# Two experts' second weights loaded in uneven row pieces, with tiny transfers between them

## The chip, the cores and the metric

The kernel runs on one core of a Trainium2 chip. The metric is the device time of one execution in microseconds (us): the median before is 178.28 us over three runs (178.04 to 178.61). A core has a matrix engine (TensorE, PE in the profile), a vector engine (VectorE, DVE), an activation engine (ScalarE, ACT), GpSimd (POOL), a queue engine (SyncE, SP), and 16 DMA engines that move data between the chip's main memory and the on-chip buffer of 128 partitions (rows).

## The reference

The reference does windowed attention for a batch of 8 with 8 heads, 576 positions and head size 64. Heads 0 to 3 see a plain window of 32 positions, heads 4 to 7 see 32 positions with a step of 4. The attention output is read as 4608 rows `x` of 512, and goes through a "soft" mixture of 8 experts with 4 slots each:

```
logits = x @ phi                       # 4608 x 32
d = softmax over the rows;  slot_input = d.T @ x     # 32 slots x 512
for e in range(8):                     # 4 slots of expert e
    h = relu(slot_input[e] @ w1[e])    # 512 -> 1024
    slot_out[e] = h @ w2[e]            # 1024 -> 512
c = softmax over the slots;  out = c @ slot_out      # 4608 x 512
```

All inputs and the output are float32 in main memory. The weights `w1` and `w2` take 2 MB per expert each, 33.6 MB together.

## The kernel before, in words

The work has two stages. First the attention of the eight batches, software-pipelined: a list of small steps written out by hand (`ORDER`) is run once per iteration, each step for the batch that its stage number gives. TensorE does scores, products and transposes, ScalarE the exponentials and many copies, VectorE the masks, 32x32 transposes and normalizations. Along the way the sums for the slots are collected. Then, once, the experts run on the 32 slots (`hps` at L608, `so` at L641), and the result is multiplied out to the 4608 output rows (L664), scaled on ScalarE and VectorE by turns (L673, L677), and stored (L686, L713).

Nearly all transfers are issued by GpSimd (`nc.gpsimd.dma_start`), in program order on one queue, and convert float32 to float16 on the way in. Every one of them covers 128 partitions, or 64 in the two last stores. In order: the raw q, k and v of each batch (L201, 1.2 MB of float32 each), with the weights `w1` of experts 0 to 4 put between them one at a time (L207), then `w1` of experts 5 to 7 as one transfer (L207), `w2` of experts 0 to 2 as one transfer (L212), `w2` of experts 3 to 5 as one transfer (L212, into space that the raw buffers leave), and `w2` of experts 6 and 7 in column halves (`load_half`, L220: one transfer per half for expert 6, two for expert 7). Last come the 17 stores of the output. The tile for `w2` of experts 0 to 2 is `w_0`; partition p holds, for each expert, 8 rows of `w2` one after the other, 4096 numbers, 16 KB in main memory and 8 KB on chip.

The list of weights that are loaded early is `EARLY`, and `load_weights` (L483) takes it off from the front. Its last entry, `(2, 0, 3)`, is the transfer that the change touches. It is issued when the raw v of the last batch has been issued (`loads`, L527). Completion of GpSimd's transfers is counted on eight semaphores, taken in turn: a transfer that comes to a semaphore waits, on GpSimd, until the one eight places before it has landed. The 16 DMA engines each write one completion mark of 4 bytes per transfer.

The order in which the experts are used is fixed at L690 to L708: experts 0 to 3, then 4 and 5, then the first column half of 6 and 7, then the first column half of the first output batches, with the second half of experts 6 and 7 put between them.

Of the kernel before, what the change touches and what calls it, by code (L numbers as in the profile page):

```python
# [10 lines left out]
FP16 = mybir.dt.float16  # L11
# [13 lines left out]
DMODEL = H * D  # L25
E_EXP = 8
S_PER_E = 4
N_SLOTS = 32
# [16 lines left out]
    (("P", 3), ("P", 4), ("L", 0), ("L", 1), ("D", 0)),  # L45
    (("D", 1), ("D", 2), ("D", 3)),
)
ORDER = """
MD0.2 MK2.2 AP4.2 ET.3 VBc.1 S1.1 MK0.1 RP4.2 ED.3 E1.1 AD1.2 EP.3 VC.1 RD1.2 MP4.2
VCc.1 ER.3 MD1.2 AD3.2 VA.1 QT0.0 AP3.2 RD3.2 VAc.1 QT1.0 RP3.2 MD3.2 S2.1 KT1.0  # L50
# [3 lines left out]
"""  # L54
STEPS = [(w.split(".")[0], int(w.split(".")[1])) for w in ORDER.split()]
ON_ACT = ('D3', 'P0', 'P1', 'P3')
# [40 lines left out]
def kernel(  # L97
# [10 lines left out]
    nc = tc.nc  # L108
# [5 lines left out]
    consts = ctx.enter_context(tc.tile_pool(name="consts", bufs=1))  # L114
# [3 lines left out]
    ident = cst[:, o : o + 128]  # L118
    spread = cst[:, o + 128 : o + 256]
    quad = cst[:, o + 256 : o + 260]  # L120
    masks = consts.tile([128, NMASK], FP16, name="masks")
    phi_raw = consts.tile([128, 4, N_SLOTS], FP16, name="phi_raw")
    phi4 = consts.tile([128, 4, 4, N_SLOTS], FP16, name="phi4")
# [14 lines left out]
    def weights_tile(pool, which, e0, e1):  # L138
        n = (4 * FDIM, 8 * DMODEL)[which - 1]
        t = pool.tile([128, e1 - e0, n], FP16, name=f"w{which}_{e0}", tag=f"w{which}_{e0}")  # L140
        for e in range(e0, e1):
            of = t[:, e - e0]
            if which == 1:
                w1t[e] = of.rearrange("p (c f) -> p c f", c=4)
            else:
                w2t[e] = of.rearrange("p (c n) -> p c n", c=8)
        return t

    EARLY = [(1, e, e + 1) for e in range(5)] + [(1, 5, 8), (2, 0, 3)]
    early_tiles = {x: weights_tile((w1_pool, w2a_pool)[x[0] - 1], *x) for x in EARLY}  # L150
# [54 lines left out]
    def load_full(t, which, e0, e1):  # L205
        if which == 1:
            nc.gpsimd.dma_start(  # L207
                out=t.rearrange("p e (u x) -> p (e u) x", u=2),
                in_=moe_w1[e0:e1].rearrange("e (u p c) f -> p (e u) (c f)", u=2, p=128),
            )  # L210
        else:
            nc.gpsimd.dma_start(  # L212
                out=t, in_=moe_w2[e0:e1].rearrange("e (p c) n -> p e (c n)", p=128)
            )

    def load_half(e, s, n):
        src = moe_w2[e].rearrange("(p c) n -> p c n", p=128)
        cols = slice(DH * s, DH * s + DH)
        for u in range(0, 8, n):
            nc.gpsimd.dma_start(out=w2t[e][:, u : u + n, cols], in_=src[:, u : u + n, cols])  # L220
# [249 lines left out]
    for which in "QK":  # L470
        load_raw(which, 1)
    nc.gpsimd.dma_start(
        out=phi_raw.rearrange("p (u c) s -> p u (c s)", u=2),
        in_=moe_phi.rearrange("(u p c) s -> p u (c s)", u=2, c=2),
# [8 lines left out]
    def load_weights(n):  # L483
        for _ in range(n):
            x = weights.pop(0)
            load_full(early_tiles[x], *x)

    tmp = {}

# [37 lines left out]
    def loads(which, b):  # L527
        load_raw(which, b)
        if which == "V":
            if b > 2:  # L530
                load_weights(1)
            if b == B - 1:
                load_weights(len(weights))
# [6 lines left out]
    for it in range(B + max(s for _, s in STEPS)):  # L540
        for op, stage in STEPS:
            b = it - stage
            if not 0 <= b < B:
                continue
            step(op, b)
            if op in frees and b + 2 < B:
                loads(frees[op], b + 2)
            left.discard((op, b))
            if w2b_pool is None and not left:
                raw_pool.release()  # L550
                w2b_pool = tc.alloc_tile_pool(name="w2b", bufs=1, side="right")
                late = weights_tile(w2b_pool, 2, 3, 6)
                slab_weights(6, "qk0", QK_SLAB)
                slab_weights(7, "qk1", QK_SLAB)
                load_full(late, 2, 3, 6)
                for s in range(2):
                    for e in (6, 7):
                        load_half(e, s, 8 if e == 6 else 4)
        if it == 0:
            nc.vector.tensor_copy(  # L560
                out=phi4, in_=phi_raw[:, :, None, :].broadcast_to([128, 4, 4, N_SLOTS])
            )
# [40 lines left out]
    for fc in range(2):  # L603
        for g in range(2):
            for dc in range(4):
                for j in range(4):
                    e = 4 * g + j
# [9 lines left out]
    for c in range(8):  # L617
# [3 lines left out]
        out=hTm[:, 0].rearrange("p c (j s) -> p c j s", j=4)[:, :, :, 0:16], in_=hT4[:, :, :, 0:16]  # L621
    )
    nc.scalar.copy(
        out=hTm[:, 1].rearrange("p c (j s) -> p c j s", j=4)[:, :, :, 16:32], in_=hT4[:, :, :, 16:32]
# [87 lines left out]
    for e in range(2):  # L712
        nc.gpsimd.dma_start(  # L713
            out=rest[:, e, 512:576, :].rearrange("n i d -> i n d"), in_=om_l[64 * e : 64 * e + 64]
# [37 lines left out]
```

## Time and profile before

| | |
|---|---|
| Median of three runs | 178.28 us |
| Profiled execution, its own time | 178.29 us |
| Its span (first to last instruction) | 176.5 us |
| Around the span | 1.79 us |
| TensorE / VectorE / ScalarE / GpSimd busy | 70% / 71% / 70% / 22% |
| Packets of GpSimd's queue | 18816, 40.41 MB written |
| Read from main memory / written to it | 62.07 MB / 9.44 MB |

The profile is one execution. "DMA" in its slices is the mean busy share of the 16 DMA engines. Each transfer of 128 rows is cut into packets, the same number for each DMA engine; an engine's packets follow each other without a hole as long as its queue holds work. Each transfer has 16 completion marks in the trace, one from each engine, and it has landed with the last of them. The trace does not number the engines: it tells that 16 marks came, and when, but not from which engine each came.

### The profile page before, as it was taken

The page shows a single profiled execution, that of the slowest core. Times are in us where ns is not written, and L with a number is a line of the kernel's source. Part 1 is how long each engine was busy: PE and PEld are TensorE (multiplying, and loading weights), DVE is VectorE, ACT ScalarE, POOL GpSimd, SP SyncE. Part 2 cuts the span into 40 slices and gives each one's busy share as a digit, 9 for nine tenths or more (in the row PEclk, how much of TensorE's full clock was granted, in tenths as well). Part 3 has the DMA queues.
Part 4 walks back from the last instruction along what each step waited for, and adds up shares of the span by engine and source line. Part 5 has one row for each costly group of instructions (what it writes and reads, how often), then busy time and mean ns, then how long its engine had stood idle before and what let it go on. Part 6 is the DMA issues. An engine that isn't in the chain of part 4 may idle for free.

```text
span 176.5 us, 4724 instructions
## 1 busy us (share of the span) xinstructions
PE 123.5 (70%) x2004; PEld 80.9 (46%) x2004; DVE 126.0 (71%) x275; ACT 123.5 (70%) x266; POOL 38.4 (22%) x60
## 2 busy tenths in 40 slices
PE   0026928998888888988989888978677295778300
PEld 0015616676566566656766557656332142221000
DVE  6473899999999999999999998465130104878500
ACT  6007758999999999999999999995501104888300
POOL 7321022112112112116000002710000001856600
PEclk9999999969999999999789999996858969655555
DMA  5999999999999999999999999999999999999997
GB/s 83 215 214 210 214 212 215 215 213 214 216 212 217 211 218 215 208 215 220 213 211 217 213 218 216 222 210 225 213 213 221 192 198 175 340 398 397 401 415 209
DMA packets 18981, 40.83 MB, mean 231 GB/s; under 512 B 1169, under 2 KB 11537, under 8 KB 18193
## 3 DMA queue, kind: packets, MB, share of 16 engines
q0 software_dynamic: 18816, 40.41, 113.8%
q8 instruction: 15, 0.25, 0.5%
q1 hardware_dynamic: 144, 0.14, 0.3%
q14 instruction: 6, 0.04, 0.1%
HBM read 62.07 MB, written 9.44 MB: 405 GB/s over the span
## 4 chain that ended last, share of the span: by engine, by line
ACT 38%; DMA 27%; DVE 14%; PE 10%; issue 2%; POOL 2%; POOLq 0%; ACTq 0%
DMA w<-in_moe_w_dram 19%; ACT p L282 10%; DMA phi_raw<-in_moe_phi_dram 8%; ACT vX L253 7%; ACT xp L337 7%; DVE qk L231 5%; PE f L664 5%; ACT om L673 3%; ACT xT L376 3%; ACT xT L378 3%; DVE p L293 3%; DVE vT L231 3%; ACT xd L337 2%; PE s L273 2%; PE rp L357 2%
## 5 line engine op out<-in xcount | busy, mean ns | idle before, releaser
L282 ACT ACTIVATE p<-s 128x1920 f16<-128x1920 f32 (+1 forms) x24 | 44.6, 1857 | 10.2 <-PE s L273 10.1
L273 PE MATMUL s<-qk 32*128 32x128 f16 (+2 forms) x704 | 26.7, 295 | 18.4 <-DVE qk L231 12.0
L253 ACT COPY vX<-rv 128x768 f16<-128x768 f16 (+1 forms) x32 | 27.8, 943 | 1.8 <-PE rv L247 1.8
L316 PEld LDWEIGHTS <-p 128*128 128x128 f16 (+1 forms) x480 | 22.4, 103 | 13.3 <-DVE xp L341 4.0
L337 ACT ACTIVATE xp<-o_P,rc_P 128x64 f16<-128x64 f32 x96 | 26.5, 497 | 2.2 <-DVE rc_P L328 2.2
L273 PEld LDWEIGHTS <-qk 32*128 32x128 f16 x704 | 17.3, 117 | 21.6 <-DVE qk L231 12.0
L293 DVE TENSOR_TENSOR p<-p,masks 128x1920 f16<-128x1920 f16 (+1 forms) x24 | 25.7, 1084 | 0.2
L231 DVE STREAM_TRANSPOSE qk<-rawQ 128x576 uint32<-128x576 uint32 x16 | 18.8, 1243 | 2.7 <-DMA rawQ<-in_q_dram 2.7
L316 PE MATMUL o_P<-vX,p 128*128 128x65 f16 (+1 forms) x288 | 20.0, 205 | 0.8 <-ACT xp L337 0.2
L231 DVE STREAM_TRANSPOSE qk<-rawK 128x576 uint32<-128x576 uint32 x16 | 19.5, 1231 | 0.4 <-DMA rawK<-in_k_dram 0.4
L247 PE MATMUL rv<-cst,vT 128*128 128x128 f16 x176 | 17.5, 242 | 3.2 <-DVE vT L231 1.8
L231 DVE STREAM_TRANSPOSE vT<-rawV 128x576 uint32<-128x576 uint32 x16 | 19.4, 1223 | 0.5 <-DMA rawV<-in_v_dram 0.5
L686 POOL DMA_DIRECT2D out_dram<-om x15 | 11.1, 744 | 39.2 <-DVE om L677 34.8
L247 PEld LDWEIGHTS <-vT 128*128 128x128 f16 x176 | 13.2, 124 | 7.5 <-issue 3.7
L677 DVE TENSOR_SCALAR om<-f,rrow 128x256 f16<-128x256 f32 (+1 forms) x28 | 13.5, 519 | 3.5 <-PE f L664 2.9
L664 PE MATMUL f<-so_sb,ET 32*128 32x256 f16 (+1 forms) x60 | 12.5, 392 | 3.9 <-ACT om L673 2.7
L673 ACT ACTIVATE om<-f,rrow 128x256 f16<-128x256 f32 (+1 forms) x28 | 12.8, 503 | 2.6 <-PE f L664 2.0
L376 ACT COPY xT<-rp 128x576 f16<-128x576 f16 x16 | 11.5, 909 | 1.3 <-PE rp L357 1.3
L316 PE MATMUL o_D<-vX,p 128*128 128x65 f16 x128 | 9.9, 202 | 2.5 <-DVE xp L341 2.0
L201 POOL DMA_DIRECT2D rawQ<-in_q_dram x8 | 5.1, 633 | 29.4 <-DVE rc_P L328 18.4
L378 ACT COPY xT<-rd 128x576 f16<-128x576 f16 x16 | 10.6, 795 | 0.0
L341 DVE TENSOR_TENSOR xd<-o_D,rc_D 128x256 f16<-128x256 f32 x24 | 9.9, 412 | 0.2
(81 smaller groups left out, 176.7 us busy)
## 6 DMA issues: line engine op xcount, KB each, us to landing
w<-in_moe_w_dram POOLq DMA_DIRECT2D x3, 3072.0 KB, 35.5
out_dram<-om POOLq DMA_DIRECT2D x11, 512.0 KB, 4.6
w<-in_moe_w_dram POOLq DMA_DIRECT2D x5, 1024.0 KB, 15.9
rawQ<-in_q_dram POOLq DMA_DIRECT2D x8, 576.0 KB, 12.7
rawK<-in_k_dram POOLq DMA_DIRECT2D x8, 576.0 KB, 11.4
rawV<-in_v_dram POOLq DMA_DIRECT2D x8, 576.0 KB, 11.6
out_dram<-om POOLq DMA_DIRECT2D x2, 1024.0 KB, 7.3
w<-in_moe_w_dram POOLq DMA_DIRECT2D x2, 512.0 KB, 36.7
```

What stands on the lines that cost most here:

```text
L231: nc.vector.transpose(out=out_, in_=in_)
L247: nc.tensor.transpose(rg[:, n_t, :, c, :], rows, ident)
L253: copy(out=vX[b % 2][:, t0 : t0 + n, :, 0:D], in_=rg.rearrange("p n h c d -> p n h (c d)"))
L273: nc.tensor.matmul(sps[:, h, c0 : c0 + w], kk, qq, start=(tt == 0), stop=(tt == 1))
L282: return nc.scalar.activation(out=pt, in_=sps[:, :, 0:n], func=AF.Exp, scale=SCALE)
L293: return nc.vector.tensor_tensor(out=pt, in0=pt, in1=m, op=ALU.mult)
L316: nc.tensor.matmul(o[rows, h, :], lhs, rhs, start=(n == 0), stop=(n == len(jobs) - 1), skip_group_check=True,)
L337: nc.scalar.activation(out=dst[:, h], in_=src[:, h], func=AF.Copy, scale=rc[:, h : h + 1])
L376: copy(out=xT_t[b][:, c, :], in_=rg[:, 0:S])
L378: copy(out=xT_t[b][:, 2 + c, :].rearrange("p (i r) -> p i r", r=DIL), in_=rg[:, :, 0:SUB].rearrange("p r i -> p i r"),)
L664: nc.tensor.matmul(fp[:, 0 : c1 - c0], ET[32 * j : 32 * j + 32, m : m + 128], so_sb[32 * j : 32 * j + 32, c0:c1], start=True, stop=True,)
L673: nc.scalar.activation(out=dst, in_=fp[:, 0 : c1 - c0], func=AF.Copy, scale=rrow[:, blk : blk + 1])
```

## The change

The single transfer for `w2` of experts 0 to 2 becomes eight transfers. Expert 0 is loaded alone, as before, in 128 rows. Experts 1 and 2 together are loaded as: 112 rows, whole; the second half of each of the last 16 rows; the first half of rows 112 to 119; the first half of rows 120 to 127. Around the last two stand three tiny transfers (`step_cursor`) of 3, 8 and 5 rows, each row two pieces of 32 numbers read from `phi`, into a new tile `aside` that nothing reads. The same bytes of `w2` arrive in the same places; all other transfers and all work on the other engines stay as they are.

```diff
+CURSOR = 3
...
+    aside = consts.tile([16, 3, 2, N_SLOTS + 16], FP16, name="aside")
...
+    def step_cursor(i, n):
+        nc.gpsimd.dma_start(
+            out=aside[0:n, i, :, 0:N_SLOTS],
+            in_=moe_phi[0 : 5 * n].rearrange("(p u) s -> p u s", u=5)[:, 0:4:2, :],
+        )
+
+    def load_uneven(t, e0, e1):
+        src = moe_w2[e0:e1].rearrange("e (p c) n -> p e (c n)", p=128)
+        half = 4 * DMODEL
+        nc.gpsimd.dma_start(out=t[0:112], in_=src[0:112])
+        nc.gpsimd.dma_start(out=t[112:128, :, half:], in_=src[112:128, :, half:])
+        step_cursor(0, CURSOR)
+        nc.gpsimd.dma_start(out=t[112:120, :, 0:half], in_=src[112:120, :, 0:half])
+        step_cursor(1, 8)
+        nc.gpsimd.dma_start(out=t[120:128, :, 0:half], in_=src[120:128, :, 0:half])
+        step_cursor(2, (-CURSOR - 24) % 16)
...
             x = weights.pop(0)
-            load_full(early_tiles[x], *x)
+            which, e0, e1 = x
+            if which == 1:
+                load_full(early_tiles[x], 1, e0, e1)
+            else:
+                load_full(early_tiles[x][:, 0:1], 2, e0, e0 + 1)
+                load_uneven(early_tiles[x][:, 1:], e0 + 1, e1)
```

## The prediction, made before the changed kernel ran

> **What bounds the kernel now.** I read the page first: the slices, the queues, the chain.
>
> ```profile
> DMA  5999999999999999999999999999999999999997
> GB/s 83 215 214 210 214 212 215 215 213 214 216 212 217 211 218 215 208 215 220 213 211 217 213 218 216 222 210 225 213 213 221 192 198 175 340 398 397 401 415 209
> ...
> q0 software_dynamic: 18816, 40.41, 113.8%
> q8 instruction: 15, 0.25, 0.5%
> ...
> ACT 38%; DMA 27%; DVE 14%; PE 10%; issue 2%; POOL 2%; POOLq 0%; ACTq 0%
> ```
>
> The chain names ScalarE most, but the DMA row is full from the second slice to the last. The engines never run dry before the last weights: a raw load waits 11.4 to 12.7 us from issue to landing while landings of neighbours are 2.7 us apart, so there is always a backlog. The last third of the chain says it directly (the chain from 104 us on; start, length, what):
>
> ```profile
> 112.33 34.05 DMA w<-in_moe_w_dram
> 146.41 0.32 PE so L641 x4
> ...
> 166.34 0.63 POOL out_dram L713
> 166.97 0.63 POOLq L747
> ```
>
> TensorE has the slots' hidden values at 138.4 us and waits for expert 7's first half, which lands at 146.4. The stores follow (the DMA view from 149.4 us to the end):
>
> ```profile
> DMA  7799999999999999999999999999999999999000
> GB/s 103 110 336 382 384 404 401 399 407 402 404 387 401 387 408 387 401 390 404 389 405 390 402 387 408 396 426 417 414 408 423 417 402 420 408 417 327 12 0 0
> ...
> out_dram<-om_l POOLq DMA_DIRECT2D x2, 512.0 KB, 8.0
> ```
>
> The last store is issued at 166.97 and lands at 175.23 us: again a backlog. So the end is the time that the busiest DMA engines need for all their bytes. The share of 7 in the first two of these slices is the point of this case: around 149 to 150.7 us some engines have nothing to do while others still load weights.
>
> The completion marks in the trace show it. For the last weight transfer (last mark at 151.70 us) the 16 engines' marks lie before it by 2.65, 2.46, 2.45, 2.38, 2.37, 2.11, 1.89, 1.52, 1.48, then 0.43, 0.41, 0.32, 0.28, 0.27, 0.20 and 0 us: nine early, seven late. At 20.9 us all were within 0.45. In between, each of the fifteen 16 KB instruction packets (the q8 row above, each 0.89 to 1.07 us long) set one engine back by about 1.1 us. The first eight of them hit eight different engines, and from the ninth (86.1 us) on one after the other is hit again, seven by the end. So there are seven engines with two fetches, one with one, eight with none; the five 8 KB packets of another instruction queue (0.32 us each) explain the steps among the early ones. The late seven have no pause from the first load to the last store; after 152.5 us all 16 are within 0.7 us and end so.
>
> **The change part by part.**
>
> *The rows.* Before, each engine gets 8 rows times 3 experts, 24 packets of 8 KB. Such a packet takes 625 ns and the next begins 19 ns before its end: 0.606 us each, 14.54 in all (landings 111.91 to 126.47 us: 14.56). A 4 KB packet takes 324, so a step of 0.305. After: 8 packets for expert 0, 14 for the 112 rows, 2 half packets for the 16 half rows: 22 x 0.606 + 2 x 0.305 = 13.94 us on all engines. Each 8-row piece can occupy at most eight engines with whole rows, 2 half packets (0.61 us) each. If both fall on the same eight, these have 15.16 us: +0.62 against before, the other eight -0.60.
>
> *The marks.* Seven more transfers, each with a mark on every engine. A mark takes 22 ns, the step is 21: 7 x 0.021 = +0.15 us on every engine. The other bound is from expert 6's half in one transfer (2.63 us between landings) against expert 7's in two (1.31 + 1.33): 0.01 each, 0.07 in all. I take 0.15, as the step is seen packet by packet.
>
> *The tiny rows.* 16 rows of two 64-byte packets. The nearest row is `phi_raw`: 128-byte packets of 32 ns, 13 ns from one to the next. If two rows fall on each of eight engines, 4 packets: 0.05 to 0.13 us; I take 0.09, and below nothing is excluded, as they are added bytes.
>
> [...]
>
> *GpSimd's queue.* Seven more issues of about 0.8 us beside it:
>
> ```profile
> 81.33 0.81 POOL L212 DMA_DIRECT2D w<-in_moe_w_dram  x1
> 105.57 0.77 POOL L212 DMA_DIRECT2D w<-in_moe_w_dram  x1 [23.43 <-DVE rc_P L328]
> 106.34 0.90 POOL L220 DMA_DIRECT2D w<-in_moe_w_dram  x1
> 111.58 3.85 POOL L220 DMA_DIRECT2D w<-in_moe_w_dram  x5 [4.34 <-PE s L273]
> ```
>
> They fall into the 23.4 us hole after 81.33. But the semaphores are taken in turn of eight, so waits move: the 5-row transfer waits for `w1` of experts 5 to 7 (landing 111.9), experts 3 to 5 behind it for expert 0 (about 116.8 instead of issue at 105.6), expert 6 for the 112 rows (about 125.2), and the six issues of the last weights end near 130 instead of 115.4. All queued behind is weights and stores; the engines have work until 141.1 from experts 3 to 5, so 11 us of cover remain. Cost nothing; without that cover each us of delay would be one of the end.
>
> *Sum.* An engine that is not picked: -0.60 + 0.15 + 0.09 = -0.36 us. A picked one: +0.62 + 0.15 = +0.77. The early ones can bear that (least lead 1.48); a late one can't. So the time goes by whether the eight picked are all early ones.
>
> *Which eight.* The trace doesn't number engines, so I use order. Chains of packets (next start = end - 19 ns) can be followed from the first transfer, with ties. The engine of the first fetch is the 13th (by other readings of ties 5th or 9th) to begin the first transfer, that of the second the 15th, of the third the 11th, of the fourth the 16th or 12th (or 4th): the hit engines seem to lie among the later eight. If the 3-row transfer takes places 1 to 3 of that order, the 8-row pieces take 4 to 11, and the 11th is a late engine. Blindly laid, eight neighbours out of 16 miss all late ones in one or two positions of 16. Two weak arguments to the same side: I take at least one late engine as picked. With the very last that is +0.77; with the next, which lead by 0.20 to 0.43, +0.34 to +0.57. Several are likely, so +0.6: 178.29 + 0.6 = 178.9 us (the profiled execution's 178.29 is 0.01 over the median).
>
> **The rivals.**
>
> *All picked are early.* Then the late engines gain 0.36 through the weights and stay without pause through the stores: 177.9 us; bounds 177.7 (mark at 0.01, tiny rows at 0.05: -0.48) to 178.0, or 177.6 if the tiny rows fall elsewhere and first stores start sooner too. For it: nine early engines are there, with at least 1.48 us to give. Against it: the order above. It decides if no late engine is among the eight.
>
> *Rows go to fixed engines from the first on, whatever came before.* Then tiny rows and pieces all fall on the first eight; if the later eight are the fetched ones, these gain 0.60 - 0.15 = 0.45: 177.8 us. Against it: no transfer before has under 64 rows, so nothing shows it.
>
> [...]
>
> *Waits or fixed costs bite.* The moved waits, or a cost per short transfer that the backlog doesn't hide: 0.1 to 0.3 us each, 7 of them, 179.0 to 180.4 us. Against it: 11 us of cover and the expert 7 pair.
>
> **How the numbers follow.** Late engine picked 0.50 (178.6 to 179.1); all early 0.36 (177.6 to 178.1); fixed first eight 0.08; waits or costs 0.06. A change of 0.3% is 0.53 us, about what measurement can tell from none: faster is under 177.75, slower over 178.81. Faster: 0.4 of the second case and 0.6 of the third, about 0.20; slower: 0.8 of the first, the fourth, 0.46; same 0.34. The range runs from the gain's lower part to the picked last engine: 177.7 to 179.1. The forecast's own range is 178.6 to 179.1.
>
> **What would show it.** The marks of the last weight transfer: the forecast has the last one later than 151.70 by some 0.6 us, with one or several marks standing out behind the rest; the rival has nine marks closer to the end by 1.1 and the last near 151.3. The transfers of experts 0 to 2 should have 352 packets of 8 KB and 64 of 4 KB in place of 384 of 8 KB. GpSimd's issue of experts 3 to 5 near 116.8. Stores should keep their distance to the last weight. Wrong would be: fetches that hit other engines than before, or a store stage that waits for something else than DMA.

## The result, and the profile after

The changed kernel takes 179.56 us (median of four runs, 179.49 to 180.10), the kernel before, on the same chip, 178.16 us: a ratio of 1.0079 with a 95% interval of 1.0060 to 1.0097. It is slower by 1.4 us. The forecast was 178.9, 0.6 us slower, with a range up to 179.1; the kernel became slower as forecast, but by more than twice as much, and for another reason, as the experiments show.

The profiled execution took 180.1 us with a span of 178.2. Its page, at the lines that were shown of before (the busy share and rate of the DMA engines in 40 slices, the queues, the chain by engine):

```profile
DMA  5999999999999999999999999999999999999997
GB/s 86 211 213 212 218 209 213 214 216 215 218 209 216 212 214 217 215 213 214 213 215 214 216 217 219 222 213 205 167 215 215 197 199 168 320 398 397 402 414 207
...
q0 software_dynamic: 19088, 40.41, 113.7%
q8 instruction: 15, 0.25, 0.5%
...
DMA 44%; DVE 19%; ACT 17%; PE 8%; POOL 4%; issue 3%; POOLq 0%
```

The bound is the one that the prediction named: the DMA row is full throughout. But the rate falls to 167 GB/s in the 29th slice (124.7 to 129.2 us), where before it was 213, and the engines are no less busy in it. The chain from 104 us on (start, length, what) shows where it leads:

```profile
81.96 44.86 DMA w<-in_moe_w_dram
...
127.72 0.38 POOL w L239
...
129.39 18.68 DMA w<-in_moe_w_dram
...
148.11 0.32 PE so L665 x4
...
168.00 0.63 POOL out_dram L737
168.64 0.64 POOLq L771
```

The transfer that starts it is the 112 rows; expert 7's first half arrives at 148.1 instead of 146.4, and everything behind it is late by about as much. From the last mark of the weights to that of the stores it is 23.53 us before and 23.52 after: the stores neither lost nor gained. So the loss is there by the last weight transfer, whose marks lie before the last one, at 153.36 us, by 3.57, 3.45, 3.43, 2.88, 2.53, 2.47, 2.37, 1.42, 1.38, 1.11, 1.01, 0.99, 0.84, 0.32 and 0.01 us. The last is 1.66 us later than the 151.70 of before, and the mean over the 16 went from 150.37 to 151.63, by 1.26.

The slices from 149.4 us to the end begin as before, with engines that have nothing to do while others load weights (the busy share of 5 in the fourth):

```profile
DMA  9985999999999999999999999999999999999100
GB/s 167 132 110 74 319 372 350 400 408 397 408 397 401 391 401 390 404 393 394 398 391 404 391 402 390 404 404 424 415 404 421 424 415 407 412 410 373 26 0 0
```

A window of 3 us over the dip gives, in its last two columns, the summed DMA share and the rate. Before:

```profile
124.00:127.00 3.00, 1.95 (x32) 1.09 (x28) 0.43 (x2) 1.79 (x4) 0.00 (x0) 1.00 1.05 218
```

After:

```profile
124.00:127.00 3.00, 1.81 (x29) 1.15 (x30) 0.55 (x2) 1.06 (x3) 0.00 (x0) 0.80 1.21 147
```

The engines hold packets for a longer time (1.21 against 1.05 of all time) and move a third less. The trace's packets of GpSimd's queue, by the microsecond in which they begin, show how (mean and longest, in ns):

```
us       before, 8 KB     after, 8 KB      after, 4 KB
123      625   625        625   625        323   324
124      625   625        736   985        352   547
125      625   625       1251  1431        559   714
126      625   625       1164  1527        855   956
127      625   625        648   794        384   494
```

From 124.2 to 127.4 us packets take up to two and a half times as long, those of 4 KB nearly three times. Summed over what a packet takes elsewhere (625 and 324 ns) that is 20.4 us of packet time between 112 and 150 us, against 0.5 before, or 1.2 us on each of 16 engines.

Most of the long packets aren't those of rows 112 to 127. The half rows of these partitions are the 64 packets of 4 KB, and the 41 of them that begin before 124.6 us take 322 or 324 ns, as elsewhere. The 39 long packets of 8 KB (over 640 ns) are other loads'. Experts 0 to 2 have 352 packets of that size, and 357 had begun by 124.24 us, before the first long one. Followed from packet to packet, some nine of these were already experts 3 to 5, so only about four of the 39 can be experts 0 to 2. Nearly all belong to the load behind, experts 3 to 5 in 128 rows. What is slow is everything in flight while the short pieces are being written, and just after: every 8 KB packet that begins from 124.39 to 127.25 us takes 661 ns or more.

### The profile page after: what moved, and what is told of

The parts are those of the page before. It is cut to its first block, busy times and chain, and to the rows that moved or that the text cites. A ratio compares the mean times of both kernels' runs of the same rounds, so it can differ in the third digit from the quotient of the medians.

```text
span 178.2 us, 4732 instructions
## 1 busy us (share of the span) xinstructions
PE 122.0 (68%) x2004; PEld 80.5 (45%) x2004; DVE 126.0 (71%) x275; ACT 123.5 (69%) x266; POOL 42.4 (24%) x67
## 4 chain that ended last, share of the span: by engine, by line
DMA 44%; DVE 19%; ACT 17%; PE 8%; POOL 4%; issue 3%; POOLq 0%
DMA w<-in_moe_w_dram 36%; DMA phi_raw<-in_moe_phi_dram 8%; DVE qk L250 7%; PE f L688 4%; DVE vT L250 4%; ACT om L697 3%; ACT p L301 3%; ACT vX L272 3%; DVE p L312 3%; ACT xp L356 3%; ACT xT L395 2%; DVE xd L360 1%; ACT xT L397 1%; ACT xd L356 1%; POOL w L209 1%
## 5 line engine op out<-in xcount | busy, mean ns | idle before, releaser
L301 ACT ACTIVATE p<-s 128x1920 f16<-128x1920 f32 (+1 forms) x24 | 45.3, 1888 | 10.4 <-PE s L292 10.3
L272 ACT COPY vX<-rv 128x768 f16<-128x768 f16 (+1 forms) x32 | 28.6, 976 | 1.7 <-PE rv L266 1.7
L356 ACT ACTIVATE xp<-o_P,rc_P 128x64 f16<-128x64 f32 x96 | 27.2, 525 | 2.0 <-DVE rc_P L347 2.0
L665 PE MATMUL so<-w,hTm 128*32 128x512 f16 (+1 forms) x80 | 6.6, 449 | 6.0 <-DMA w<-in_moe_w_dram 5.5
```

The source lines that it names most:

```text
L272: copy(out=vX[b % 2][:, t0 : t0 + n, :, 0:D], in_=rg.rearrange("p n h c d -> p n h (c d)"))
L301: return nc.scalar.activation(out=pt, in_=sps[:, :, 0:n], func=AF.Exp, scale=SCALE)
L356: nc.scalar.activation(out=dst[:, h], in_=src[:, h], func=AF.Copy, scale=rc[:, h : h + 1])
```

## The experiments

Each diff is against the changed kernel, unless it says otherwise. "Stretch" is the sum just defined, over the same 112 to 150 us (0.5 us before, 20.4 in the changed kernel); "marks" are those of the last weight transfer. The kernel before took 178.3 us beside e1 to e12, 178.6 beside e13 to e16 and 178.5 beside e17 and e18.

### Is it the engines that are picked, the tiny transfers, or the last rows? (e1 to e4)

e1 is meant to move the pick to the other eight engines, by a larger first tiny transfer. Which engines a given number of tiny rows picks is my assumption, here and in e9 to e18; no run shows it.

```diff
-CURSOR = 3
+CURSOR = 11
```

> The two 8-row pieces are meant to move to the other eight engines (the first tiny transfer has 11 rows, the last 13). Theory A, a late engine was picked in the change: now the picked ones would be the other eight; if those are all early, the time falls to 177.9 to 178.3 us, and the last weight's mark to about 151.3. Theory B, the pile-up: in the changed kernel packets of 8 KB stretched from 625 ns to as much as 1527 between 124.2 and 127.4 us, while 16 engines wrote rows 112 to 127; this doesn't depend on the pick, so some 0.8 us stay: 178.7 to 179.6 us, with stretched packets again.

179.88 us, ratio 1.0079 (1.0061 to 1.0097), above both expected ranges. The loss is the same. Stretch 14.6 us, last mark 153.67. The pick alone doesn't make the loss.

e2 leaves the tiny transfers out:

```diff
-        step_cursor(0, CURSOR)
...
-        step_cursor(1, 8)
...
-        step_cursor(2, (-CURSOR - 24) % 16)
```

> The three tiny transfers are left out, so the two 8-row pieces should fall on different eights and all engines carry the same bytes, four marks more than before. Theory A (picks): no imbalance is left, 178.3 to 178.4 us. Theory B (pile-up on rows 112 to 127): the stretched packets stay, 178.9 to 179.3 us.

179.48 us, 1.0068 (1.0053 to 1.0083); stretch 16.4. The tiny transfers aren't the cause either.

e3 loads the last 16 rows as one transfer of whole rows, so that every engine should have the same bytes and nothing is picked:

```diff
-        nc.gpsimd.dma_start(out=t[112:128, :, half:], in_=src[112:128, :, half:])
...
-        nc.gpsimd.dma_start(out=t[120:128, :, 0:half], in_=src[120:128, :, 0:half])
-        step_cursor(2, (-CURSOR - 24) % 16)
+        nc.gpsimd.dma_start(out=t[112:128], in_=src[112:128])
```

> Experts 1 and 2 as 112 rows and 16 rows, both whole, nothing else: two marks more than before, no imbalance, no 8-row piece, no tiny transfer. Theory A: 178.2 to 178.4 us. Theory B: 16 engines still write 16 neighbouring rows at once, packets stretch, 178.9 to 179.6 us.

179.73 us, 1.0082 (1.0066 to 1.0098), with a stretch of 16.2 us. This is the whole loss without anything uneven. The same window as above, of e3:

```profile
124.00:127.00 3.00, 1.81 (x34) 1.10 (x32) 0.55 (x2) 1.30 (x3) 0.00 (x0) 1.00 1.13 167
```

The rate is 167 GB/s where before had 218. Here, too, most of the long packets are those behind: by the same count some 50 of the 71 long ones of 8 KB that begin between 123.9 and 127.9 us belong to experts 3 to 5. What the short transfer itself shows is late landing. The 32 completion marks of the 112 and the 16 rows reach their semaphores 0.95 us on average after their 4-byte packets; for the one transfer of experts 0 to 2 before it is 0.30. In the changed kernel the first 41 packets of 4 KB take 322 or 324 ns, and the long packets follow, up to 1527 ns. The trace doesn't show where they wait.

e4 keeps only the split into expert 0 and experts 1 and 2, both of 128 rows:

```diff
-        nc.gpsimd.dma_start(out=t[0:112], in_=src[0:112])
...
-        step_cursor(2, (-CURSOR - 24) % 16)
+        nc.gpsimd.dma_start(out=t, in_=src)
```

> Expert 0 alone and experts 1 and 2 together, both in 128 rows: one mark more than before. Both theories: 178.1 to 178.4 us and no stretched packet. A time over 178.8 would say that the splitting by itself, or the wait of experts 3 to 5 for expert 0's semaphore, costs.

178.52 us, 1.0005 (0.9994 to 1.0015); stretch 0.5. So the split is free, and the loss comes with the transfers of the last 16 rows.

### Short transfers, rows read, or rows written? (e5 to e8)

Four kernels load experts 1 and 2 in eight transfers of 16 rows. They differ in which partitions a transfer writes (16 neighbours, or every 8th) and which rows it reads (16 neighbours in main memory, or every 8th). e6 and e7 thereby leave the rows in another order than the reference has them; bytes and work are the same.

```diff
-        nc.gpsimd.dma_start(out=t[0:112], in_=src[0:112])
...
-        step_cursor(2, (-CURSOR - 24) % 16)
+        for r in range(8):
+            nc.gpsimd.dma_start(out=t[16 * r : 16 * r + 16], in_=src[16 * r : 16 * r + 16])    # e5
+            nc.gpsimd.dma_start(out=t[16 * r : 16 * r + 16], in_=src[r:128:8])                 # e6
+            nc.gpsimd.dma_start(out=t[r:128:8], in_=src[16 * r : 16 * r + 16])                 # e7
+            nc.gpsimd.dma_start(out=t[r:128:8], in_=src[r:128:8])                              # e8
```

> Experts 1 and 2 in eight transfers of 16 neighbouring rows, from 16 neighbouring rows of w2 to 16 neighbouring partitions: the crowd of the 16-row piece eight times over, with nothing uneven. Theory C (the writes crowd: 16 engines into few neighbouring partitions) and theory D (the reads crowd: 16 engines read one block of neighbouring rows in memory) both expect stretched packets in all eight: the 9.7 us that the 16 packets of an engine take stretch by 1 to 10 us, 180 to 188 us. A time under 178.9 would say that it isn't the 16 neighbouring rows but what stands before or behind them. [...]

> Left out: the right order of the rows of experts 1 and 2 (rows r, r+8, r+16 and so on of w2 come into 16 neighbouring partitions). Neighbours are written, rows 128 KB apart are read. Theory C (writes crowd): as slow as the transfers from neighbouring rows to neighbouring partitions, 180 to 188 us. Theory D (reads crowd): 178.3 to 178.7 us, no stretched packets.

> Left out: the right order of the rows of experts 1 and 2 (16 neighbouring rows of w2 come into every eighth partition). Every eighth partition is written, neighbours are read. Theory C (writes crowd): 178.3 to 178.9 us, few or no stretched packets (8 marks more than before are 0.17 us). Theory D (reads crowd): 180 to 188 us.

> Experts 1 and 2 in eight transfers of 16 rows, every eighth row to every eighth partition. Both theories: 178.3 to 178.9 us, few or no stretched packets. If it is slow too, transfers of 16 rows cost by themselves (one row and engine, many marks), whatever rows they are.

| | writes | reads | us | ratio (95%) | stretch, us | GB/s, 124 to 127 us |
|---|---|---|---|---|---|---|
| e5 | neighbours | neighbours | 181.87 | 1.0188 (1.0158 to 1.0217) | 40.2 | 167 |
| e6 | neighbours | every 8th | 181.28 | 1.0155 (1.0051 to 1.0258) | 54.9 | 131 |
| e7 | every 8th | neighbours | 178.49 | 1.0005 (0.9989 to 1.0022) | 0.3 | 216 |
| e8 | every 8th | every 8th | 178.52 | 1.0012 (1.0001 to 1.0024) | 0.3 | 218 |

The window of e6 and that of e7, where neighbours and every 8th change places between the writes and the reads:

```profile
124.00:127.00 3.00, 1.81 (x31) 1.08 (x30) 0.55 (x2) 1.33 (x3) 1.38 (x2) 0.92 0.95 131
```

```profile
124.00:127.00 3.00, 1.81 (x29) 1.13 (x30) 0.55 (x2) 1.04 (x3) 1.92 (x3) 0.80 1.04 216
```

It is the writes. Eight transfers of 16 rows cost 0.2 us by the medians, 0.4 at most by the intervals, as long as each spreads its rows over the partitions; the same bytes into 16 neighbouring partitions at a time cost 3.6 and 3.0 us (e5 and e6, two runs each). Where the rows are read makes no loss by itself. In e5 the 8 KB packets have means of 655 to 931 ns, by the microsecond, from 117 to 129 us; in e7 and e8 only a few leave 625.

The crowd slows more than the weights. In e5 and e6 the 16 KB instruction packet at 117 us took 1306 and 1284 ns, in e7 and e8 893 and 962; the 8 KB instruction packet at 124 us took 820 and 1021, against 322 (at 122 us) in e7 and e8. These packets carry no row of the weights.

In e7 and e8, with every 8th partition, an 8 KB packet takes 625 ns but for a few. In e5, where every packet of experts 1 and 2 goes to neighbours, the worst mean is 931 ns, and the 1251 ns of the changed kernel are mostly packets of another load. No run here shows why neighbours cost; the runs show that 16 neighbours cost and every 8th partition doesn't.

### What the pick is worth without the crowd (e9 to e18)

With this the prediction's own term, which engines get the pieces, could be tried without the crowd. e9 to e12 load the even part as 64, 32 and 16 rows at steps of 2, 4 and 8, and the pieces into partitions 0, 8, ... 120, with first tiny transfers of 3, 7, 11 and 15 rows.

```diff
-CURSOR = 3
+CURSOR = 3    # e9; 7 in e10, 11 in e11, 15 in e12
...
-        nc.gpsimd.dma_start(out=t[0:112], in_=src[0:112])
-        nc.gpsimd.dma_start(out=t[112:128, :, half:], in_=src[112:128, :, half:])
+        for first, step in ((1, 2), (2, 4), (4, 8)):
+            nc.gpsimd.dma_start(out=t[first:128:step], in_=src[first:128:step])
+        nc.gpsimd.dma_start(out=t[0:128:8, :, half:], in_=src[0:128:8, :, half:])
...
-        nc.gpsimd.dma_start(out=t[112:120, :, 0:half], in_=src[112:120, :, 0:half])
+        nc.gpsimd.dma_start(out=t[0:64:8, :, 0:half], in_=src[0:64:8, :, 0:half])
...
-        nc.gpsimd.dma_start(out=t[120:128, :, 0:half], in_=src[120:128, :, 0:half])
+        nc.gpsimd.dma_start(out=t[64:128:8, :, 0:half], in_=src[64:128:8, :, 0:half])
```

> The same uneven load of experts 1 and 2 with the same three tiny transfers, but the 112 rows as 64, 32 and 16 rows at steps of 2, 4 and 8, and the pieces from and to every eighth row, so that no transfer writes neighbours. Nine marks more than before (0.19 us). Theory C: no stretched packets, and what is left is the forecast's sum: an engine that isn't picked -0.32 us, a picked one +0.81. The changed kernel's tiny rows lay on five early and three late engines, so four late ones are picked: last weight's mark 0.3 to 0.8 us later than before, 178.6 to 179.1 us. If packets stretch as before: 179.3 us and more.

> As with the spread rows and a first tiny transfer of 3 rows, but 7 (the last then has 1 row). If the late engines stand next to each other in the order, four places on, either all or none of the picked ones are late: 177.9 to 178.2 us, or 178.6 to 179.1. If the order doesn't matter, as with 3.

> Spread rows, first tiny transfer of 11 rows: the other eight are picked than with 3, among them three late ones, and more tiny rows: 178.6 to 179.2 us.

> Spread rows, first tiny transfer of 15 rows: the other eight than with 7. If 7 picks the late ones, this picks the early ones and the time falls to 177.9 to 178.2 us; if 7 picks the early ones, this rises to 178.6 to 179.1.

181.75, 182.04, 181.91 and 181.74 us; ratios 1.0195 (1.0175 to 1.0215), 1.0214 (1.0196 to 1.0232), 1.0209 (1.0179 to 1.0240) and 1.0182 (1.0150 to 1.0213). All are slower than expected, by a new cause. GpSimd's queue in e9 from 112 us (start, length; in brackets the wait before and what ended it):

```profile
112.29 0.55 POOL L219 DMA_DIRECT2D aside<-in_moe_phi_dram  x1 [14.20 <-DMA w<-in_moe_w_dram]
117.04 0.54 POOL L233 DMA_DIRECT2D w<-in_moe_w_dram  x1 [4.20 <-DMA w<-in_moe_w_dram]
121.90 0.56 POOL L219 DMA_DIRECT2D aside<-in_moe_phi_dram  x1 [4.33 <-DMA w<-in_moe_w_dram]
124.98 0.78 POOL L214 DMA_DIRECT2D w<-in_moe_w_dram  x1 [2.52 <-DMA w<-in_moe_w_dram]
```

With ten transfers in place of eight the load of experts 3 to 5 (the last line) meets the semaphore of the 32 rows, which land at 124.10 us. It is issued at 124.98 instead of 117.26, when the engines have next to nothing left: its first packet is at 126.47, and the window shows a busy share of 0.67 and 103 GB/s:

```profile
124.00:127.00 3.00, 2.25 (x31) 1.52 (x29) 0.05 (x1) 1.85 (x4) 1.95 (x3) 0.50 0.67 103
```

This is the rival of the moved waits, not in the change but two transfers further. The first 8 KB packets after the pause took up to 1345 ns in e9, and the stretch of these four kernels is 8.4 to 10.0 us: packets are long after a pause, too, without neighbours being written, so a long packet alone doesn't name its cause. One thing can be read beside it: the last packet of experts 0 to 2 and of the tiny rows ended at 126.92, 127.11, 126.59 and 125.78 us for 3, 7, 11 and 15 rows. So the pick seems to move the late engines by over 1 us, and 15 looks like the one that spares them.

e13 to e15 issue the pieces after experts 3 to 5 instead (15 rows, 7 rows, and no tiny transfers):

```diff
+    def load_pieces(t, e0, e1):
+        src = moe_w2[e0:e1].rearrange("e (p c) n -> p e (c n)", p=128)
         half = 4 * DMODEL
...
+                load_pieces(early_tiles[(2, 0, 3)][:, 1:], 1, 3)
```

> Spread rows, first tiny transfer of 15 rows, and the uneven pieces issued behind the load of experts 3 to 5, so that the engines don't run dry while GpSimd waits for a semaphore (in the four spread versions experts 3 to 5 were issued near 125 us, and fewer than 4 packets were in flight near 126). With 15 the pieces' last packet ended at 125.78 us, 0.69 before the end of experts 0 to 2 in the kernel before. Theory E (the forecast's sum holds once nothing crowds and nothing runs dry): the late engines gain 0.3 to 0.6 us, 177.6 to 178.0 us, last weight's mark near 151.2. If it is 178.2 or more, the balance of the engines isn't worth what the marks and tiny rows cost.

> The same with a first tiny transfer of 7 rows, which picks the other eight. Theory E: late engines are picked, +0.5 to +0.8 us: 178.8 to 179.2 us. The same time as with 15 would say that the pick doesn't matter.

> The same without tiny transfers, so that all engines carry the same bytes: the price of the six more marks and of the other order alone. Theory E: 178.3 to 178.6 us, between the two others.

179.97 us, 1.0083 (1.0067 to 1.0099); 179.82, 1.0067 (1.0048 to 1.0086); 178.52, 0.9998 (0.9987 to 1.0010). The first two are 2 and 0.6 us above what was expected. In e13 the wait only moved: the last five loads stood behind the landing of experts 3 to 5 and were issued at 140.42 us,

```profile
140.42 3.87 POOL L243 DMA_DIRECT2D w<-in_moe_w_dram  x5 [13.65 <-DMA w<-in_moe_w_dram]
```

and the engines ran dry at 141 to 142 and at 145 to 147 us. Nothing can be read from these two on the pick. e15, with spread rows, three transfers fewer and no uneven load, is the kernel before again.

e16 gives the changed kernel itself the pick of 15 rows:

```diff
-CURSOR = 3
+CURSOR = 15
```

> The changed kernel itself, with a first tiny transfer of 15 rows in place of 3 (neighbouring rows, old order). Theory B and E together: the crowd on rows 112 to 127 stays (stretched packets, about +1.2 us as with 112 and 16 whole rows), the pick gives some 0.4 to 0.6 back: 178.7 to 179.3 us.

180.08 us, 1.0078 (1.0055 to 1.0100); stretch 18.5. The expected gain is missing: under the crowd the pick makes no difference that can be told, as in e1.

e17 and e18 take away both the crowd and the late issue. All of experts 0 to 2 is loaded in spread rows and the last tiny transfer is left out, so that there are eight transfers, as in the change. The picked engines have half as much again to carry as in the change.

```diff
-CURSOR = 3
+CURSOR = 15    # e17; 7 in e18
...
-        step_cursor(2, (-CURSOR - 24) % 16)
...
-                load_full(early_tiles[x][:, 0:1], 2, e0, e0 + 1)
-                load_uneven(early_tiles[x][:, 1:], e0 + 1, e1)
+                load_uneven(early_tiles[x], e0, e1)     # rows as in e9
```

> Uneven rows without the crowd: all of experts 0 to 2 as 64, 32 and 16 rows at steps 2, 4 and 8, then halves of rows 0, 8, ... 120, with a first tiny transfer of 15 rows and a second of 8; no third one. Eight transfers, as many as the change, so the load of experts 3 to 5 waits only for the 64 rows (landing near 119.3 us), 7 us before the engines could run dry. An engine not picked has 21 x 0.606 + 0.92 = 13.64 us against 14.54, with marks and tiny rows -0.7; a picked one +1.1. With the first tiny transfer of 15 rows the packet ends of the earlier runs say that early engines are picked. Theory (bytes of the late engines decide, the crowd was the loss): the pick now shows, last weight mark near 151.1, 177.6 to 178.0 us, excess packet time under 3 us. Rival (any uneven or sub-16-row transfer costs by itself, wherever it writes): 179 us or more.

> The same with a first tiny transfer of 7 rows: by the packet ends of the earlier runs late engines are picked, these have +1.1 us. Theory: last weight mark near 152.5, 179.0 to 179.5 us, over 1 us behind the kernel with 15, without any crowd of packets. Rival (the pick never decides): both kernels the same within 0.3%.

e17: 178.99 us (178.91 to 179.38), 1.0034 (1.0021 to 1.0047). e18: 179.49 (179.22 to 180.25), 1.0068 (1.0049 to 1.0087). The stretch is 0.7 and 0.3 us, the load of experts 3 to 5 is issued at 120.2 and 119.7, and the window of e17 has its rate:

```profile
124.00:127.00 3.00, 1.77 (x30) 1.07 (x30) 0.56 (x2) 1.52 (x4) 1.66 (x2) 1.00 1.10 219
```

e18 came out as expected (last mark 152.69). The two differ by 0.5 us with intervals that only just don't overlap, in the pick and in eight tiny rows: the pick seems to count, by about half of what was expected. e17 missed its gain, and its marks show how. At the transfer that landed at 144.64 us, 14 marks lay within 1.1 us: the late engines had been relieved. At the next, at 147.11, one stands 1.07 us behind all others, and it stays there to the last weight (152.45; the next at 151.31). Between the two lies the 15th instruction packet, at 144.5 us. I read it so that this engine is one of those that fetch, and was among the picked. That isn't shown engine by engine, as the trace doesn't number them. Without that set-back the last mark would be 0.39 us earlier than before. By their times alone both kernels also fit the rival set against e17, that any uneven or short transfer costs by itself (179 us or more); against it stand the missing stretch, and a mean mark that is only 0.31 and 0.20 us later than before.

## Why the prediction was wrong, point by point

**The bound held.** The time goes by the last mark of the weights plus 23.4 to 23.9 us of stores, in the profiled execution of the kernel before, of the changed one and of all experiments. The step from bytes to end was right.

**The failing step is the rows.** It took 0.606 us for every whole row and 0.305 for every half row, wherever they are written, and so "13.94 us on all engines". These prices come from transfers of 128 rows. The 16 neighbouring rows added a cost that the sum puts at nothing: while they were being written, and just after, packets of whatever load took up to 1527 ns (8 KB) and 956 ns (4 KB), 1.2 us on each engine. By the sum, the mean of the 16 engines had to move by (-0.36 + 0.77) / 2 = +0.2 us; it moved by 1.26. Where the rows are spread, in e17 and e18, the sum asks for +0.2 again ((-0.7 + 1.1) / 2), and the mean moved by 0.31 and 0.20: without the crowd the sum fits. e3 shows the cause alone, with the same loss and nothing uneven, and e8 shows short transfers of spread rows without it. The step bounded marks, tiny rows and waits from both sides, but not this: no row of the trace of before had a transfer of 16 rows, which was said of the pick and not of the price. That the kernel became slower, as forecast, is luck: the forecast's reason was a late engine that is picked, and e3, which picks none, loses as much.

**The marks and the tiny rows were small, as forecast.** e8 has eight transfers more than before, the change seven; its mean mark moved by 0.17 us, 0.021 for each, as forecast. The match to the third digit is luck, as one profile each scatters by as much: the mean moved by 0.25 in e7 with eight more as well, by 0.18 in e4 with one more, and by 0.02 in e15 with six more. e2 without tiny rows stays within 0.1 us of the change.

**The packets and the issues came nearly as forecast.** The 352 packets of 8 KB and 64 of 4 KB are there; experts 3 to 5 are issued at 117.26 (forecast 116.8), and the last six issues end at 132.5 (forecast near 130; the 112 rows that they wait for land at 126.8 instead of 125.2):

```profile
97.47 0.55 POOL L232 DMA_DIRECT2D w<-in_moe_w_dram  x1 [4.65 <-DMA w<-in_moe_w_dram]
112.41 0.57 POOL L219 DMA_DIRECT2D aside<-in_moe_phi_dram  x1 [14.39 <-DMA w<-in_moe_w_dram]
117.26 0.79 POOL L214 DMA_DIRECT2D w<-in_moe_w_dram  x1 [4.28 <-DVE rc_P L347]
127.72 4.80 POOL L239 DMA_DIRECT2D w<-in_moe_w_dram  x6 [9.67 <-DMA w<-in_moe_w_dram]
```

The waits are long (14.4 and 9.7 us) and the engines never ran dry behind them. But the cover was thinner than it looks. With two transfers more, in e9, the kernel was 3.5 us slower than before and 2.2 us slower than the changed one. The forecast's "each us of delay would be one of the end" points the right way there; that the price is one for one isn't measured.

**The pick.** Eight engines carry the tiny rows twice over, and these packets come in groups: five engines at 122.9 to 124.4 us and three at 125.9 to 126.2. So the eight that got the pieces, the others, seem to hold four of the seven late ones, as the forecast took it to be. That a pick of late engines costs fits e18 against e17. In the change, though, this term can't be told apart: e1 and e16, meant to pick others, and e3, which picks none, lose as much. The +0.6 isn't what the time shows. It also rests on an order in which the tiny rows take the first places and the pieces the next, and no run shows that order. What the runs show in its place is the two groups of tiny packets, the ends from 125.78 to 127.11 us in e9 to e12, and the 0.5 us between e17 and e18.

**The rivals.** "All picked are early" and "fixed first eight" gave times that didn't come, though the crowd hides what the pick alone would have done. Against "fixed first eight" stands that the groups of tiny packets seem to lie on other engines than the pieces. "Waits or fixed costs bite" gave the right time (179.0 to 180.4) by luck: the waits let no engine run dry in the change, and e8 shows no such cost of a short transfer by itself. The cost hangs on which partitions it writes.

What stays open: why neighbouring partitions cost, how the crowd slows packets that write elsewhere, and whether a pick of early engines alone would beat the kernel before. No kernel tried does; e15 and e4, the best, are the kernel before within their intervals.

## What to carry to other kernels

When a load is cut into pieces, look at which partitions are written at the same time: for some 3 us pieces of 16 neighbouring rows lost a quarter to a third of the rate here (167 and 147 GB/s against 218), pieces of every 8th row nothing. Don't carry a packet's price from a 128-row transfer to a short one (625 ns before, means up to 931 in e5), and look for the loss in the load behind it, too. And count transfers against the eight semaphores: each one more moves a later load's issue behind an earlier landing (with two more, in e9, that of experts 3 to 5 from 117.26 us to 124.98, behind a landing at 124.10), free of charge until the engines run dry, and then at a price (3.5 us in e9).

## What the runs showed of the hardware

- An 8 KB packet takes 625 ns where 16 engines write spread partitions (before, e7, e8). While and just after they write 16 neighbouring ones, packets of other loads are long as well: up to 1527 ns for 8 KB in the changed kernel, and 1306 ns for a 16 KB instruction packet in e5 (893 in e7).
- The landing of a transfer follows its 4-byte packets by 0.30 us before, and by 0.95 on average for the 112 and 16 rows of e3.
- Eight more transfers of 16 rows in a backlogged queue moved the mean mark by 0.17 us in all (e8), 0.25 in e7.
- After the engines had run dry, the first packet came 1.5 us after the issue began (124.98 to 126.47 us, e9).
- The instruction packets' durations repeat with a period of eight (in the changed kernel 949, 945, 935, 974, 974, 961, 893, 893 ns, and then 948, 945 and so on). The kernel before has the same set from another place on, but for two longer packets (935, 974, 974, 1074, 893, 893, 948, 945, then 935, 974, 975, 961, 1011, 893, 948). So one set of eight engines seems to fetch in turn, and a late packet may undo what was gained by sparing one of them, as I read e17.
